# The last row's second layer in two groups of four K/V heads, each with its own softmax, under new instruction orders

## Chip, cores and metric

The kernel runs on one core of one Trainium2 chip. The metric is the device time of one execution in microseconds (us); lower is better. A time is given as the median of several executions, and one further execution was profiled.

## What is computed

Eight rows (one token each) go through four blocks: attention over a window of a K/V cache, a dense block, the same attention again with the same weights and caches, and the same dense block again. The window is the last 1024 of 4096 positions; there are 16 query heads and 8 K/V heads of 256 columns, so two query heads share a K/V head.

```python
def _A_ref(x, k_cache, v_cache, wq, wo):
    W = min(4096, max(256, Sk // 4))                     # 1024
    q = (x @ wq).reshape(B, Sq, Hq, Dh)...               # 8, 1, 16, 256
    k = jnp.repeat(k_cache[:, :, Sk - W:, :], rep, axis=1)
    v = jnp.repeat(v_cache[:, :, Sk - W:, :], rep, axis=1)
    p = _softmax(jnp.einsum("bhqd,bhkd->bhqk", q, k) * (Dh ** -0.5))
    return jnp.einsum("bhqk,bhkd->bhqd", p, v)... @ wo

x = x + _A_ref(_layernorm(x), A_k_cache, A_v_cache, A_wq, A_wo)
x = x + _B_ref(_layernorm(x), B_w1, B_w2)                # silu(x @ w1) @ w2
x = x + _A_ref(_layernorm(x), A_k_cache, A_v_cache, A_wq, A_wo)
x = x + _B_ref(_layernorm(x), B_w1, B_w2)
```

All data is bf16. K and V of the windows are 67 MB, the weights another 10.5 MB, and everything is read once.

## The kernel before, in words

**Stages of a row.** Each row b has two passes, called layer 1 and layer 2, that use the same K and V in SBUF. K/V pieces (512 KB each, 8 of K and 8 of V for a row) are loaded by SyncE into a ring of 30 slots (`load_kv`, L453; the order and the reuse of slots in `pump`, L1034). A slot is loaded again when the row's layer 2 has used it: K slots after the layer-2 scores, V slots after the layer-2 products with V. So TensorE's progress opens the gate for the loads of the next row but one.

- VectorE transposes K in place, two halves of each piece, 16 per row (`KT`, L630).
- Scores: TensorE multiplies the query blocks with K, in two halves of four K/V heads each (`S`, L645; 64 matmuls per layer and row, named S0 for layer 1 and S1 for layer 2, with .0 and .1 for the two halves). Both halves go into one PSUM bank, bank 0 for layer 1 and bank 1 for layer 2.
- Softmax (L654 to L676): VectorE takes the maximum and spreads it (max, mT, mg, mb: L658 to L662), ScalarE the exponential (`exp`, L664), TensorE a permutation (`perm`, L666), VectorE a transpose (`turn`, L668); TensorE sums the denominators (`l`, L671) and VectorE inverts them (`rl`, L676).
- Products with V (PV, L709 and L728), copies out of PSUM (`oev`, L698 and L703), a turn by matmuls with the identity (`oT`, L689), the division (`oTev`, L683), the product with wo (L781), a copy to a row (`rowb`, L1063), a fold of it into columns (`fold`, L499).
- Statistics of the row (`stat`, L814; `var`, L817; `pow`, L819), w1 (L516), a transpose (`yT`, L536), tanh (L826), `hT` (L827), w2 (L845), the same fold again, then the query product with wq (L872), its transpose (`qT`), `qm` (L881), `qd` (L885) and the query blocks for layer 2 (`qbd2`, L889).

Layer 1 of row b+1 needs only the input, so its scores, softmax and V products are woven between the stages of layer 2 of row b. For rows 0 to 6 the last output product and the second dense block are done together at the end (`final_rows`, L892), beside the last row's own chain; the last row is finished by `final_last` (L977). In the last row, layer 2's scores of all eight K/V heads go into bank 1, one softmax follows, then the V products of both halves, four copies of them on ScalarE (L698), the turns, and the product with wo (L781, `woL`).

**Zero products.** `busy` (L830) issues matmuls of 512 columns on a column of zeros: 8 in row 0, 5 in every other row, 5 more at the end. Their result is not used. They stand in TensorE's order at places where it would otherwise wait.

**Start.** Before the first use of wo and w2, sums of their rows are formed (`row_sums`, L426): three- and two-block reductions on VectorE (L435) and single ones on ScalarE (L443), with their writers L438 and L447. ScalarE loads its function table once at the start, and a second time by an explicit instruction (L328).

**Order.** Every engine runs its instructions in a fixed order. The steps are first listed in program order; the table `ORDER` (L16) then holds for each engine a string of digits, each of which says which of the steps that are left comes next. Waits on other engines are added by `emit` (L108). Nothing is chosen at run time: a step that waits holds up all that stands behind it on its engine.

Of the kernel before, what the change touches and what calls it, by code (L numbers as in the profile page):

```python
# [17 lines left out]
        "000000011111l111133312223022051002010033300710500300111117777000440033333210011004403330201101044000"  # L18
        "1770000300111117777000400444423010011155510022011101044000177005000011111777700040044442320001115514"
        "0022201101044000177710000011111777700040044442320001161514002201110004400017716111101111177770004004"  # L20
        "4442320001161510022201110105400017771000001111177770004004444232000116151002201111010033001777710100"
        "ccc0b1111060000444442200011817771002022220000033ccc43a02060500001140333333300110000022220b1200000000"
        "11000"),
    "dve": (
        "pSG0G0bGq0njnwvZtutFtUEg4CQz0g4yBydzjhvHwbvnFrEAAzkayz352iuj9k6q935nikb8g14f2a4439nj90888c8685c09664"
        "4551122baaa2a929216bd1aaa10077700555555000010098880870705ac09a90087700555550000100098880870705ac09aa"
        "0077700555550000100a08880878060aab09a0087700555550000100098880870705aa0aa90077700555550000100a088808"
        "78060aab0990087700555550000100098880778060acb0b99a900005555500000000099ag90ebb8ba8006004403020100001"
        "111100000000"),
    "act": (  # L30
        "13333442444455f5e56432322224222111111113312211111111111331211111111111133122111111111113312211111111"
        "11133122100000000000220111000000000302011000000004002200010010000000"),
    "pool": (
        "00010011022002200200020002000010001000"),
# [167 lines left out]
def bass_interleave_layers__sliding_block_cached__dense_activation_silu__decode_kernel(  # L202
# [429 lines left out]
    def scores(b, layer, k2):  # L632

        sc = bank[SC[layer]]
        q = qbd[layer][:]
        up_to = 8 if k2 else 16
        for cb in range(4):
            fns = []
            for par in range(2):
                for j in range(4):  # L640
                    a = 16 + 256 * k2 + (j * 8 + cb * 2 + par) * 8
                    w = q[:, a - up_to:a]
                    kv = slots[slot_of[b, "k", 4 * k2 + j]][:, :].rearrange(
                        "p (u cb jj par) -> p cb par u jj", u=8, cb=4, par=2)[:, cb, par, :, :]
                    fns.append(lambda e, w=w, j=j, kv=kv, cb=cb, par=par: e.matmul(  # L645
                        sc[32 * j:32 * j + up_to, 0:256], w, kv, start=(cb == 0 and par == 0),
                        stop=(cb == 3 and par == 1), tile_position=(0, 32 * j), skip_group_check=True))
            pe(fns, [k for j in range(4) for k in SL(slot_of[b, "k", 4 * k2 + j])] + [("pad", layer)] + QB(layer, k2),
               bk(SC[layer]), b, "S%d.%d" % (layer, k2))
# [4 lines left out]
    def softmax(b, L):  # L654
        m, tb = mm[L], LB[L]
        x = bank[SC[L]][:, 0:256]
        l_ps = bank[SC[L]][:, 256:256 + H]
        dve(lambda e: e.tensor_reduce(m[:, 0:1], x, AX.X, ALU.max, negate=True), bk(SC[L]), [("mm", L)], b, "max%d" % L)  # L658
        dve(lambda e: e.transpose(m[:], m[:]), [("mm", L)], [("mm", L)], b, "mT%d" % L)
        dve(lambda e: e.tensor_reduce(mg[L][:, 0:4], m[:, 0:16].rearrange("p (n q) -> p n q", q=4), AX.X,  # L660
                                      ALU.min), [("mm", L)], [("mg", L)], b, "mg%d" % L)
        dve(lambda e: e.transpose(m[:].rearrange("p (z n q) -> p z n q", z=2, q=4), view(mg[L][:], 0, [(0, 2), (1, 4), (0, 4)])),  # L662
            [("mg", L), ("mm", L)], [("mm", L)], b, "mb%d" % L)
        act(lambda e: e.activation(E_sb[L], x, ACTF.Exp, bias=m[:, 0:1], scale=1.0, accum_out=esum[:, L:L + 1]),  # L664
            bk(SC[L]) + [("mm", L)], QB(L, 1) + [("es", L)], b, "exp%d" % L)
        pe(lambda e: e.matmul(bank[tb][:, 0:256], perm[:], E_sb[L], start=True, stop=True),  # L666
           QB(L, 1) + PERM, bk(tb), b, "perm%d" % L)
        dve(lambda e: e.transpose(view(pT_sb[L], 0, [(64, 4), (1, 2), (2, 32)]),  # L668
                                  bank[tb][:, 0:256].bitcast(BF16)[:, 1:512:2].rearrange("p (u s n) -> p u s n", s=2, n=32)),
            bk(tb), QB(L, 0), b, "turn%d" % L)  # L670
        pe(lambda e: e.matmul(l_ps, esum[:, L:L + 1].broadcast_to([P, P]), selh[:], start=True, stop=True),  # L671
           [("es", L), "selh"], bk(SC[L]), b, "l%d" % L)
        if L == 1 and b < LAST:
            act(lambda e: e.activation(l2[b], l_ps, ACTF.Copy), bk(SC[L]), [("l2", b)], b, "lc1")
        else:
            dve(lambda e: e.reciprocal(rl[b], l_ps), bk(SC[L]), [("rl", b)], b, "rl%d" % L)  # L676

    def o_out(b, L, n, o_c, dst, h0, keys, name):
        if dst is None:
# [6 lines left out]
            bk(LB[L]) + [("rl", b)], keys, b, "oTev" + name)  # L686
# [6 lines left out]
    def o_turn(b, L, n, sel_o, o_c, dst, h0, keys, name, halves):  # L693

        ob = bank[OB[L]]
        if halves:
            for s in range(2):
                act(lambda e, s=s: e.activation(E_sb[L], ob[:, s * DH:(s + 1) * DH], ACTF.Copy), bk(OB[L]), QB(L, 1), b,  # L698
                    "oev%s.%d" % (name, s))
                o_sel(L, lambda s: E_sb[L], s, sel_o, o_c, n, QB(L, 1), b, "oT%s.%d" % (name, s))  # L700
# [4 lines left out]
        o_out(b, L, n, o_c, dst, h0, keys, name)  # L705

    def pv(b, L, j, kvh, u0, u1, c0, n, name, ob=None):

        return [lambda e, u=u: e.matmul(  # L709
            bank[OB[L] if ob is None else ob][32 * j:32 * j + 2 * n, :], pT_sb[L][:, pcol(u, c0):pcol(u, c0) + 2 * n],  # L710
# [39 lines left out]
    def pv_last2(b):  # L750
        for k2 in range(2):
            L = 1 - k2
            lists = [pv(b, 1, j, 4 * k2 + j, 0, 8, 2 + 8 * k2 + 2 * j, 2, "", OB[L]) for j in range(4)]
            for i in range(4):
                pe([l[i] for l in lists], [k for j in range(4) for k in SL(slot_of[b, "v", 4 * k2 + j])] + QB(1, 0),
                   bk(OB[L]), b, "PV1.%d" % k2)
            o_turn(b, L, 8, lambda s: view(ident[:], s, [(32, 4), (2, 2)]), C_O, oT2[b][:, :, 8 * k2:8 * k2 + 8], 8 * k2,
                   [("oT2", b, k2)], "L%d" % k2, True)
# [133 lines left out]
    def final_rows(s):  # L892
# [41 lines left out]
        for i0 in range(0, NCH, 8):  # L934
# [29 lines left out]
            bank[XB8][32 * (f % 4):32 * (f % 4) + n, 0:D], h8[:, f * n:(f + 1) * n],  # L964
            w2_sb[:, f // 2 * PW + R0 + f % 2 * D:f // 2 * PW + R0 + (f % 2 + 1) * D],
            start=(f < 4), stop=(f >= FC - 4), tile_position=(0, 32 * (f % 4)), skip_group_check=True)
            for f in range(FC)], ["h8"] + W2_R, bk(XB8), row, "w28")
# [3 lines left out]
        act(lambda e: e.activation(rb9, bank[XB8][:, 0:D], ACTF.Copy), bk(XB8) + KEY, ["rb8"], row, "rowb9")  # L971
# [158 lines left out]
```

## Time and profile before

| | us |
|---|---|
| median of 3 runs (235.59 to 236.86) | 236.27 |
| the profiled execution | 235.61 |
| its span in the profile | 233.7 |
| TensorE busy | 168.2 (72%) |
| VectorE busy | 155.3 (66%) |
| ScalarE busy | 68.5 (29%) |
| last K/V piece landed, about | 201 |

PE is TensorE, DVE VectorE, ACT ScalarE, POOL GpSimd, SP SyncE; SPq, PEq and so on are the engines' instruction queues. The chain of work that ended last is followed back from the last instruction: at each step to what released it, or to the instruction before it on its engine. In a timeline a row gives the start and the length in us, the engine, the line of the kernel, what is written and read, how many, and in brackets the idle time of the engine ahead of it with what ended that. The table of windows gives for each stretch its length, the busy time of each engine, TensorE's granted clock, the busy share of the DMA engines and the rate in GB/s. All times of a row count from the start of the span.

### The profile page before, as it was taken

Reading aid. Unit: us, or ns where it says so; the run is one execution under the profiler, and the core shown is the slowest. Engines: PE = TensorE matmul, PEld = TensorE weight load, DVE = VectorE, ACT = ScalarE, POOL = GpSimd, SP = SyncE. Lnnn points to the kernel's source line nnn. Section 1 sums busy time; section 2 is a strip of 40 time slices with the busy share of each in tenths; the row PEclk is TensorE's granted clock in tenths of the full one; section 3 lists DMA queues with packets and bytes.
Section 4 is the critical chain, followed back from the end, with each engine's and each line's share of the span. In section 5 each row is a group of like instructions: output and inputs, shape, how many; then the busy total and the mean of one; then the engine's idle time right before and its main releaser. Section 6 shows DMA issues by size and latency. Waiting matters only on the chain.

```text
span 233.7 us, 8070 instructions
## 1 busy us (share of the span) xinstructions
PE 168.2 (72%) x3569; PEld 93.4 (40%) x3569; DVE 155.3 (66%) x412; ACT 68.5 (29%) x205; POOL 22.8 (10%) x42
## 2 busy tenths in 40 slices
PE   0001505488788888989788898889788987999873
PEld 0001503123454455446344543644464454456441
DVE  3038999986963896488578649955974795365501
ACT  2000002896222321331332233225213322333330
POOL 1000022000300200200012001101010110012000
PEclk9999999999999999999999999999999999999999
DMA  6999999999999999999999999999999998300000
GB/s 163 413 403 407 379 381 399 407 407 412 405 403 392 414 404 356 365 414 409 400 406 406 400 400 409 409 326 407 410 406 382 411 409 329 127 3 3 3 1 4
DMA packets 23401, 78.20 MB, mean 335 GB/s; under 512 B 3127, under 2 KB 6086, under 8 KB 22982
## 3 DMA queue, kind: packets, MB, share of 16 engines
q1 hardware_dynamic: 22806, 77.30, 84.7%
q8 instruction: 28, 0.46, 0.8%
q10 hardware_dynamic: 560, 0.38, 0.8%
q14 instruction: 7, 0.06, 0.1%
HBM read 77.67 MB, written 0.01 MB: 332 GB/s over the span
## 4 chain that ended last, share of the span: by engine, by line
PE 47%; DVE 22%; DMA 13%; ACT 10%; issue 5%; SPq 2%; ACTq 0%; DVEq 0%
DMA slot<-in_A_k_cache_dram 13%; PE bank L645 11%; DVE slot L630 9%; PE bank L709 7%; PE bank L872 6%; PE bank L781 4%; DVE slot L435 3%; PE bank L845 2%; ACT qbd L664 2%; PE bank L728 2%; PE bank L516 2%; ACT slot L443 2%; PE bank L885 2%; ACT qbd L698 1%; PE bank L666 1%
## 5 line engine op out<-in xcount | busy, mean ns | idle before, releaser
L630 DVE STREAM_TRANSPOSE slot<-slot 128x512 uint32<-128x512 uint32 x128 | 81.9, 682 | 16.6 <-DMA slot<-in_A_k_cache_dram 16.3
L645 PE MATMUL bank<-slot,qbd 128*16 128x256 bf16 (+1 forms) x1024 | 40.4, 286 | 7.0 <-ACT qbd L889 3.2
L645 PEld LDWEIGHTS bank<-slot,qbd 128*16 128x16 bf16 (+1 forms) x1024 | 23.9, 88 | 17.8 <-ACT qbd L889 7.2
L709 PE MATMUL bank<-slot,qbd 128*4 128x512 bf16 (+1 forms) x384 | 27.9, 388 | 1.8 <-DVE xb L584 1.3
L819 POOL TENSOR_TENSOR fcols<-fcols 128x1 f32<-128x1 f32 x17 | 9.4, 553 | 109.6 <-ACT fcols L817 109.6
L781 PE MATMUL bank<-wo_sb,q1s 128*1 128x449 bf16 x284 | 17.0, 362 | 0.4 <-ACT wo_sb L447 0.4
L872 PE MATMUL bank<-wq_sb,xbz 128*2 128x256 bf16 x512 | 16.7, 275 | 0.1
L833 PE MATMUL bank<-ident,cols 128*128 128x512 bf16 x48 | 16.2, 391 | 0.0
L620 POOL TENSOR_TENSOR qbd<-q1s,fcols 128x256 bf16<-128x256 bf16 x16 | 9.6, 612 | 65.1 <-PE bank L689 59.1
L889 ACT ACTIVATE qbd<-bank 128x256 bf16<-128x256 f32 x16 | 6.1, 383 | 32.9 <-PE bank L885 32.9
L668 DVE STREAM_TRANSPOSE qbd<-bank 128x256 bf16<-128x256 bf16 x16 | 7.7, 478 | 12.1 <-PE bank L666 11.5
L683 DVE TENSOR_TENSOR q1s<-bank,q1s 128x16 bf16<-128x16 f32 (+1 forms) x18 | 2.9, 160 | 17.7 <-PE bank L689 17.5
L698 ACT ACTIVATE qbd<-bank 128x256 bf16<-128x256 f32 x22 | 8.3, 382 | 18.4 <-PE bank L709 16.8
L709 PEld LDWEIGHTS bank<-slot,qbd 128*4 128x4 bf16 (+1 forms) x384 | 8.1, 84 | 12.6 <-issue 2.1
L536 DVE STREAM_TRANSPOSE bank<-bank 128x256 f32<-128x256 f32 (+1 forms) x25 | 10.8, 433 | 3.6 <-PE bank L1004 1.2
L872 PEld LDWEIGHTS bank<-wq_sb,xbz 128*2 128x2 bf16 x512 | 11.4, 82 | 2.8 <-DVE xbz L807 0.4
L549 PE MATMUL bank<-xb,cols 128*128 128x8 bf16 x4 | 0.3, 173 | 16.6 <-DVE cols L331 16.6
L703 ACT ACTIVATE qbd<-bank 128x512 bf16<-128x512 f32 x14 | 8.3, 595 | 11.8 <-PE bank L728 10.9
L728 PE MATMUL bank<-slot,qbd 128*12 128x512 bf16 (+3 forms) x124 | 11.2, 408 | 0.0
L658 DVE TENSOR_REDUCE mm<-bank 128x1 f32<-128x256 f32 x16 | 6.8, 423 | 6.1 <-PE bank L645 5.4
L443 ACT ACTIVATE slot<-w_sb 128x448 bf16<-128x448 bf16 x6 | 3.5, 576 | 22.3 <-DMA w_sb<-in_B_w_dram 22.2
L845 PE MATMUL bank<-w_sb,q1s 128*1 128x449 bf16 x98 | 6.5, 353 | 4.8 <-DVE q1s L827 4.8
(158 smaller groups left out, 229.9 us busy)
## 6 DMA issues: line engine op xcount, KB each, us to landing
slot<-in_A_k_cache_dram SPq DMA_DIRECT2D x64, 512.0 KB, 8.5
slot<-in_A_v_cache_dram SPq DMA_DIRECT2D x64, 512.0 KB, 11.0
wo_sb<-in_A_wo_dram SPq DMA_DIRECT2D x1, 3584.0 KB, 25.5
wq_sb<-in_A_wq_dram SPq DMA_DIRECT2D x3, 1024.0 KB, 8.7
w_sb<-in_B_w_dram SPq DMA_DIRECT2D x1, 1568.0 KB, 27.8
w_sb<-in_B_w_dram SPq DMA_DIRECT2D x1, 1344.0 KB, 17.6
wq_sb<-in_A_wq_dram SPq DMA_DIRECT2D x1, 256.0 KB, 3.6
wq_sb<-in_A_wq_dram ACTq DMA_DIRECT2D x1, 256.0 KB, 4.0
```

What stands on the lines that cost most here:

```text
L536: dve(lambda e: e.transpose(view(bank[bi][:], n, [(2, n // 32), (n // 16, 16), (1, 2)]), bank[bi][:, 0:n].rearrange("p (g r s) -> p g r s" ...
L620: pool(lambda e, k2=k2: e.tensor_tensor(qdata(0, k2), q1s[:, b, 64 * k2:64 * k2 + 64].rearrange("p (n r) -> p n r", r=2).unsqueeze(3) .bro ...
L630: dve(lambda e, v=v: e.transpose(v, v), SL(s, h), SL(s, h), b, "KT%d" % k)
L645: fns.append(lambda e, w=w, j=j, kv=kv, cb=cb, par=par: e.matmul(sc[32 * j:32 * j + up_to, 0:256], w, kv, start=(cb == 0 and par == 0), st ...
L698: act(lambda e, s=s: e.activation(E_sb[L], ob[:, s * DH:(s + 1) * DH], ACTF.Copy), bk(OB[L]), QB(L, 1), b, "oev%s.%d" % (name, s))
L709: return [lambda e, u=u: e.matmul(bank[OB[L] if ob is None else ob][32 * j:32 * j + 2 * n, :], pT_sb[L][:, pcol(u, c0):pcol(u, c0) + 2 * n ...
L728: pe([lambda e, t=t, c0=c0, w=w, kvh=kvh: e.matmul(bank[OB[0]][32 * t:32 * t + 2 * w, :], pT_sb[0][:, pcol(2 * t, c0):pcol(2 * t, c0) + 2 ...
L781: fns.append(lambda e, i=i, w=w, c0=c0: e.matmul(bank[XB][32 * (i % 4):32 * (i % 4) + 1, c0:c0 + D + 1], oT(i), w, start=(i < 4), stop=(i ...
L819: pool(lambda e: e.tensor_tensor(rhalf, var4, nhalf, ALU.pow), ["var4", "nhalf"], ["rhalf"], b, "pow" + name)
L833: pe(lambda e: e.matmul(bank[SC[1]][:, :], cols[:, 3:4].broadcast_to([P, P]), view(ident[:], 0, [(0, 4), (1, P)]), start=True, stop=True), ...
L845: fns.append(lambda e, f=f, w=w, c0=c0: e.matmul(bank[XB][32 * (f % 4):32 * (f % 4) + 1, c0:c0 + D + 1], hTr[b][:, f:f + 1], w, start=(f < 4),
L872: pe([lambda e, j=j, c=c, s=s, wb=wb, k2=k2: e.matmul(bank[wb][32 * j:32 * j + 2, 0:256], pair(b, xcol(c, k2), s), view(wq_sb[:], c * HD + ...
```

## The change

In the last row, layer 2 is split at the half between K/V heads 3 and 4. The scores of the first half go into bank 1, those of the second into bank 0, and each half has a softmax of its own, with steps max, mT, mg, mb, exp, perm, turn, l and rl each; the denominators are kept apart. In the copies of the V products, each half's second copy moves from ScalarE to VectorE. Because bank 0 is now taken, w2 of the other seven rows (`w28`) uses bank 6. All zero products stay: 8, 5 and 5 as before. The strings of `ORDER` are new for all four engines; they move steps in every row, row 0 and the initial memsets included. Line numbers after L632 shift by 1 to 15.

```diff
-    def scores(b, layer, k2):
+    def scores(b, layer, k2, sb_i=None):
-        sc = bank[SC[layer]]
+        sb_i = SC[layer] if sb_i is None else sb_i
+        sc = bank[sb_i]
...
-    def softmax(b, L):
-        m, tb = mm[L], LB[L]
-        x = bank[SC[L]][:, 0:256]
-        l_ps = bank[SC[L]][:, 256:256 + H]
+    def softmax(b, L, g=None):
+        si, tb, qi = (SC[L], LB[L], L) if g is None else (SC[1 - g], LB[1 - g], g)
+        m, gm, E, pT = mm[si], mg[si], E_sb[qi], pT_sb[qi]
+        h0, nh = (0, H) if g is None else (8 * g, 8)
+        x = bank[si][:, 0:256]
+        l_ps = bank[si][:, 256 + h0:256 + h0 + nh]
...
     def o_turn(...)
             for s in range(2):
-                act(lambda e, s=s: e.activation(E_sb[L], ob[:, s * DH:(s + 1) * DH], ACTF.Copy), ...
+                if rk is None or s == 0:
+                    act(lambda e, s=s: e.activation(E_sb[qi], ob[:, s * DH:(s + 1) * DH], ACTF.Copy), ...
+                else:
+                    dve(lambda e, s=s: e.tensor_copy(pT_sb[qi], ob[:, s * DH:(s + 1) * DH]), ...
...
     def attend2(b):
         for k2 in range(2):
-            scores(b, 1, k2)
+            scores(b, 1, k2, SC[1 - k2] if b == LAST else None)
             freed.update((b, "k", 4 * k2 + j) for j in range(4))
             pump()
-        softmax(b, 1)
+            if b == LAST:
+                softmax(b, 1, k2)
+        if b < LAST:
+            softmax(b, 1)
```

Of `ORDER`, the first line of the string for VectorE, before and now:

```diff
-        "pSG0G0bGq0njnwvZtutFtUEg4CQz0g4yBydzjhvHwbvnFrEAAzkayz352iuj9k6q935nikb8g14f2a4439nj90888c8685c09664"
+        "nrAmnzFH.16jAv2HDvFjYuuhmCSCQsBfetOo2aIf91s944dCo26o1jdy9xk13igh59em0ak239g8g49d4838706k66696dd6ab11"
```

**VectorE, row 0.** What stands around row 0's first softmax before (L435 are the row sums of wo and w2, L658 to L662 are max to mb, L668 is turn):

```order
L435 TENSOR_REDUCE slot<-wo_sb 128x6 x2
L658 TENSOR_REDUCE mm<-bank 128x1
L331 MEMSET cols 1x1
L659 STREAM_TRANSPOSE mm<-mm 128x32
L660 TENSOR_REDUCE mg<-mm 128x4
L662 STREAM_TRANSPOSE mm<-mg 128x32
L435 TENSOR_REDUCE slot<-w_sb 128x4
L668 STREAM_TRANSPOSE qbd<-bank 128x4x2x32
```

The same place in the change (max to mb are now L663 to L667, turn is L673):

```order
L435 TENSOR_REDUCE slot<-wo_sb 128x6
L663 TENSOR_REDUCE mm<-bank 128x1
L664 STREAM_TRANSPOSE mm<-mm 128x32
L665 TENSOR_REDUCE mg<-mm 128x4
L435 TENSOR_REDUCE slot<-w_sb 128x4
L667 STREAM_TRANSPOSE mm<-mg 128x32
L435 TENSOR_REDUCE slot<-wo_sb 128x6
L438 TENSOR_SCALAR wo_sb<-slot 128x3x2
L673 STREAM_TRANSPOSE qbd<-bank 128x4x2x32
```

One of the two reductions ahead of max has moved behind mb, and the reduction of w2 from behind mb to ahead of it: between max and turn there are now two long reductions in place of one.

**TensorE, from row 6 to row 7.** Before, from the query product of row 6 (L872) to the first V products of row 7 (L709). L645 with 8x256 are here the second half of row 7's layer-1 scores, and with 16x256 and then 8x256 the two halves of row 6's layer-2 scores; L885 is qd, L666 perm of row 7's layer 1:

```order
L872 MATMUL bank<-wq_sb,xbz 2x256 x32
L645 MATMUL bank<-slot,qbd 8x256 x24
L885 MATMUL bank<-qm,spread 128x4x2x8 x4
L645 MATMUL bank<-slot,qbd 8x256 x8
L645 MATMUL bank<-slot,qbd 16x256 x32
L885 MATMUL bank<-qm,spread 128x4x2x8 x4
L666 MATMUL bank<-qbd,perm 128x256
L645 MATMUL bank<-slot,qbd 8x256 x32
L709 MATMUL bank<-slot,qbd 4x512 x16
```

In the change (L884 is the query product, L646 are the scores, L897 is qd, L671 perm, L721 the V products):

```order
L884 MATMUL bank<-wq_sb,xbz 2x256 x32
L646 MATMUL bank<-slot,qbd 8x256 x32
L897 MATMUL bank<-qm,spread 128x4x2x8 x8
L646 MATMUL bank<-slot,qbd 16x256 x32
L671 MATMUL bank<-qbd,perm 128x256
L646 MATMUL bank<-slot,qbd 8x256 x32
L721 MATMUL bank<-slot,qbd 4x512 x16
```

Both qd steps now stand together, ahead of all layer-2 scores, and nothing but perm stands between the halves of those.

**TensorE, the last row's layer 2.** Before, from the second half of the scores to the turns (L963 is w2 of the other seven rows, L968 and L972 belong to them too; L666 is perm, L671 l, L709 PV, L689 oT):

```order
L645 MATMUL bank<-slot,qbd 8x256 x32
L963 MATMUL bank<-w_sb,slot 7x448 x14
L968 MATMUL bank<-ident,slot 7x128 x3
L968 MATMUL bank<-ident,slot 7x64
L666 MATMUL bank<-qbd,perm 128x256
L671 MATMUL bank<-selh,fcols 128x16
L972 MATMUL bank<-slot 7x448
L709 MATMUL bank<-slot,qbd 4x512 x32
L689 MATMUL bank<-ident,qbd 128x8 x2
```

In the change (L671 is perm, L676 l, L721 PV, L695 oT):

```order
L646 MATMUL bank<-slot,qbd 8x256 x32
L975 MATMUL bank<-w_sb,slot 7x448 x14
L671 MATMUL bank<-qbd,perm 128x256
L980 MATMUL bank<-ident,slot 7x128 x3
L980 MATMUL bank<-ident,slot 7x64
L676 MATMUL bank<-selh,fcols 128x8
L984 MATMUL bank<-slot 7x448
L721 MATMUL bank<-slot,qbd 4x512 x4
L671 MATMUL bank<-qbd,perm 128x256
L721 MATMUL bank<-slot,qbd 4x512 x28
L676 MATMUL bank<-selh,fcols 128x8
L695 MATMUL bank<-ident,qbd 128x8 x4
```

There are two perm and two l; the second perm stands behind the first group of V products, and the turns of the first half follow together.

On ScalarE, the explicit table load (L328) moves from row 5, where it stood between the copy of the denominators (L674) and `rowb`, to row 7, between `var` (L829) and tanh (L838). In row 0, two of its reductions for w2 move from ahead of exp to behind it. On TensorE, in row 1 the turn of row 0's layer 2 (oT) stands ahead of the fold instead of behind it. In rows 2 and 3 (and, as before, row 6) the first half of the query product stands ahead of the layer-2 statistics step instead of behind it.

More of the change, by code (lines that the diff above doesn't have):

```diff
@@ L648, in scores @@
             pe(fns, [k for j in range(4) for k in SL(slot_of[b, "k", 4 * k2 + j])] + [("pad", layer)] + QB(layer, k2),
[L649 removed]
+               bk(sb_i), b, "S%d.%d" % (layer, k2))
     def pcol(u, c):
         return 64 * (u // 2) + 2 * c + u % 2
[L654 to L668 removed]
```

85 lines of the change are left out of this document (51 added, 34 removed).

## The prediction

> **What bounds the kernel now.** I read the page's shares of the chain of waits first.
>
> ```profile
> PE 47%; DVE 22%; DMA 13%; ACT 10%; issue 5%; SPq 2%; ACTq 0%; DVEq 0%
> ```
>
> Nearly half of the chain is TensorE and 13% are transfers. Two stretches of the table of windows (start:end, length, busy time of PE, PEld, DVE, ACT and POOL, granted clock, DMA share, GB/s) show what the middle rows are near to:
>
> ```profile
> 89.00:97.00 8.00, 6.64 (x125) 3.27 (x116) 3.39 (x12) 2.76 (x9) 0.00 (x0) 1.00 0.94 338
> 97.00:133.00 36.00, 31.15 (x688) 17.62 (x686) 28.17 (x66) 9.74 (x29) 4.59 (x8) 1.00 1.03 406
> ```
>
> TensorE is busy 31.15 of 36 us (87%) and the transfers run at 406 GB/s; only where slots come free late (89 to 97) do they drop to 338. A row has 16 pieces of 512 KB, 8.39 MB, which take 20.7 us at 406 GB/s. The rows follow each other at 21.2 us (the copy `rowb` of row 0 at 56.45 and that of row 5 at 162.34, both quoted below). So TensorE's order is the limit, with the transfers close behind: a shorter row cannot gain much before loading becomes the limit. SyncE's own waits say who holds the loads back (sum, number, longest):
>
> ```profile
> SPq L456 <- PE bank L645: 70.0, 12, 11.1
> ```
>
> They wait for scores, that is for TensorE to free K slots; a delay of TensorE in row 0 therefore delays loads too and is not made up by them. After about 201 us, when the last piece has landed, all is computation.
>
> **A, row 0: +1.6 (bounds +0.5 and +2.9).** The chain of waits through row 0's first softmax (start, length, engine, line):
>
> ```profile
> 36.96 5.72 DVE slot L435 x2
> 43.71 1.90 DVE slot L435
> 45.61 0.38 DVE qbd L668
> 46.04 1.45 PE bank L709 x12
> ```
>
> Before, max could start only when two reductions of wo had gone by, at 36.96 + 5.72 = 42.68, though the scores were done a little earlier. TensorE's timeline has the end of the scores, and further on row 0's two products with wo, which are needed below:
>
> ```profile
> 41.06 1.45 PE L645 MATMUL bank<-slot,qbd 128*8 128x256 bf16 x24
> ...
> 53.03 1.45 PE L781 MATMUL bank<-wo_sb,q1s 128*1 128x449 bf16 x16
> ...
> 55.46 0.93 PE L781 MATMUL bank<-wo_sb,q1s 128*1 128x449 bf16 x16 [0.41 <-ACT wo_sb L447]
> ```
>
> The scores ended at 42.51. I expect their end at about 41.1 now: the zero product of about 0.6 that stood between them is ahead of them, and VectorE hands over the query about 0.8 earlier (both estimates). From max to mb it was 42.68 to 43.71, 1.03, with 0.2 for mb: so max, mT and mg to 41.9, then the reduction of w2, 1.9, then mb, to 44.0 or 44.1. Behind mb now stands a reduction of wo, 5.72/2 = 2.9, where the shorter one of 1.9 stood: 47.0, a writer of about 0.2, and turn, 0.4, to 47.6. The V products start at 47.6 instead of 46.04: **+1.56**. ScalarE confirms it by another way:
>
> ```profile
> 42.61 0.58 ACT L443 ACTIVATE slot<-w_sb 128x448 bf16<-128x448 bf16 x1
> 43.09 0.19 ACT L443 ACTIVATION_READ_ACCUMULATOR slot<-w_sb 128x1 f32 x1
> 43.74 0.47 ACT L664 ACTIVATE qbd<-bank,mm 128x256 bf16<-128x256 f32 x1 [0.47 <-DVE mm L662]
> ...
> 56.45 0.55 ACT L1063 ACTIVATE rowb<-bank 128x450 bf16<-128x450 f32 x1 [1.13 <-PE bank L781]
> ```
>
> One of its reductions takes 0.67 with its read (42.61 to 43.28). Two of them move behind exp, 1.35 to 1.4, and exp starts at about 44.2 instead of 43.74, 0.46 later, so the last writer of wo's sums, for which the second product with wo waits (0.41 above), comes up to 1.9 later; some 0.3 of that goes into gaps between ScalarE's steps, which leaves 1.6. `rowb` would start at about 58.05, 1.6 later than before. The two ways agree, and nothing covers them: the rest of row 0 hangs on that `rowb`, and in TensorE's order row 1 begins only behind w2 of row 0. The low bound, +0.5, has only exp's own lateness (0.46) lost; the high one, +2.9, adds 1.3 for a slower TensorE. The rows for that are the zero products (line 833), by stretch:
>
> ```profile
> 50.00:54.00 4.00, 0.59 (x1) 0.10 (x1) 1.00 1.03 409
> 54.00:58.00 4.00, 1.14 (x3) 0.29 (x3) 1.00 1.03 410
> ```
>
> The same product took 0.59 in the first stretch and 1.14/3 = 0.38 in the second, at a granted clock (third number from the right) of 1.00 in both; the two products with wo above took 1.45 and 0.93 on the two sides of the change. If the lower rate of work lasted until row 0's first w1, the second product with wo would cost 0.5 more, and w1 with the zero products beside it, by the same ratio of 1.45/0.93, up to 0.8 more: together 1.3, an estimate. [...]
>
> **B, rows 1 to 5: −0.8 (0 and −1.5).** TensorE's waits at the statistics (sum, number, longest):
>
> ```profile
> PE bank L814 <- ACT q1s L867: 2.3, 5, 0.7
> ...
> PE bank L814 <- ACT q1s L680: 1.4, 5, 0.4
> ```
>
> The first row is for the layer-2 statistics, 2.3/5 = 0.46 each; the second the layer-1 statistics, 1.4/5 = 0.28 each, which wait for the copy (L680) of the turn of the row before, out of the same bank. Both together, 3.7, are the most that another order could hide. In row 1 that turn now stands ahead of the fold, so its copy is done when the statistics come: 0.3. In rows 2 and 3 half of the query product stands ahead of the layer-2 statistics and fills a wait of 0.46; `qm` needs the statistics' result, which comes later by this, so I take about half, 0.25 each. In rows 4 and 5 the same steps stand at nearly the same places. Sum −0.8. At worst it is nothing (what is put ahead delays the statistics' own chain by all that it fills); the upper end, −1.5, is 0.3 a row, since transfers of 20.7 us a row stand close behind.
>
> **C, row 6 to row 7: −0.4 (0 and −0.8).**
>
> ```profile
> 193.54 0.83 PE L645 MATMUL bank<-slot,qbd 128*8 128x256 bf16 x24 [0.70 <-DVE slot L630]
> ...
> 196.66 0.38 PE L885 MATMUL bank<-qm,spread 128*128 128x64 bf16 x4 [0.36 <-issue]
> ...
> 197.52 1.08 PE L645 MATMUL bank<-slot,qbd 128*8 128x256 bf16 x32 [0.32 <-ACT qbd L889]
> ```
>
> With both qd steps together, ScalarE's copies of the query blocks run beside the first half of the scores: the wait of 0.32 ahead of the second half and some of the 0.36 ahead of the second qd go. I take −0.4 of the 0.68; the upper end, −0.8, adds a little of the 0.70 ahead of 193.54. At the least it is nothing: both qd must now be done before any layer-2 score. VectorE puts the first transposes of row 7's K ahead of a division of row 6, which can cost 0.7 if that K lands late; the same 0.70 of idle time at 193.54 would cover it.
>
> **D, the last row's tail: −0.7 (+0.3 and −1.1).** The end of the chain:
>
> ```profile
> 216.19 1.72 PE bank L645 x52
> 217.93 0.43 DVE mm L658
> ...
> 220.61 1.93 PE bank L709 x32
> 222.56 0.39 ACT qbd L698
> 223.25 0.39 ACT qbd L698
> 223.89 1.66 PE bank L781 x24
> ```
>
> One softmax lay wholly between the scores and the V products: 217.91 to 220.61, 2.7 us. Now max of the first half starts when its 32 matmuls are through. Half of the scores is some 1.0 us (the row at 197.52), so max at about 216.95, and the same 2.7 us, with w2 of the other rows beside it, give 219.7; with 0.15 for the smaller engine order I take 219.85 for the first V products (before 220.61). Half of them last 0.97, to 220.8. The second max cannot start before the scores' end and its turn stands behind one more VectorE step:
>
> ```profile
> 220.59 0.61 DVE L974 CAST slot<-bank 7x448 bf16<-7x448 f32 x1
> ```
>
> That puts the second half's V products at 220.9, their end at 221.9 instead of 222.54, so −0.6. Of the four copies (223.25 is the last of them), half go to VectorE, beside ScalarE: the last copy ends 0.1 sooner after the products than its 1.1 us before, and the product with wo starts at about 223.1 to 223.2 instead of 223.89. **−0.7.** Added are one max, mT, mg, mb, exp, perm, turn, l and rl: some 2 us of VectorE and ScalarE, in stretches where these wait for scores anyway. Without that cover the second chain starts when the first is through with VectorE and the V products of the second half are 1 us later than taken: +0.3. The other end is −1.1, the 0.97 of one half fully hidden and 0.1 from the copies.
>
> **E, ScalarE's table load: 0 (0 and +0.43).**
>
> ```profile
> 160.56 1.28 ACT L328 ACT_TABLE_LOAD   x1
> 162.34 0.55 ACT L1063 ACTIVATE rowb<-bank 128x450 bf16<-128x450 f32 x1 [0.50 <-PE bank L781]
> ...
> 208.86 0.27 ACT L826 ACTIVATE th<-bank,fcols 128x14 f32<-128x14 f32 x1 [1.35 <-DVE bank L536]
> ```
>
> It moves to just ahead of tanh of row 7, where ScalarE waits 1.35 for w1's transpose. 1.28 fits. If what stands around it costs as much as the 0.50 left after it in row 5, 1.28 + 0.50 − 1.35 = 0.43 is late, on the path. [...]
>
> **Sum.** +1.6 − 0.8 − 0.4 − 0.7 + 0 = **−0.3** on the profiled execution's 235.61: 235.3. The median of the runs is 0.66 above that execution, so on its scale the prediction is **236.0**, by −0.3 from 236.27.
>
> **Rivals.** *R1, the delay of row 0 does not reach the end: 234.4.* Row 0's excess would be taken up if rows 1 and 2 are held by their K and V rather than by TensorE: 236.27 − 0.8 − 0.4 − 0.7 = 234.4. For it speaks the 338 GB/s at 89 to 97, a place where loads are late; against it that SyncE waits for TensorE (70.0 us over 12). *R2, slower: row 0's delay comes with longer products on TensorE and the middle rows gain nothing: 238.1.* [...] Price: 1.6 + 1.3 − 0.4 − 0.7 = +1.8, 238.1. It decides for slower as soon as these longer products cost over 0.7, with nothing from the middle rows. [...] *R3, the table load is not hidden: 237.3.* If it starts only when tanh could have started, all of its 1.28 is late: 236.0 + 1.3. Against it: in row 5 it started as soon as ScalarE was free, and 0.50 is all that is seen behind it. [...] *R4, the second softmax doesn't shorten the tail: 236.7.* This is the change not doing what it says: the second max, exp and turn are served behind the first half's on VectorE and ScalarE, so the second V products start where the only ones did, and D is 0. Against it speaks that VectorE has little else there.
>
> **How the numbers follow.** The forecast, within some 0.7 of 236.0, has 0.42; R1 0.26; R2 0.20; R4 0.07; R3 0.05. A measurement of this kernel can tell about 0.5%, 1.2 us: faster is below 235.1, slower above 237.4. R1 is faster, and 0.04 of the forecast's case: 0.30. R2 is slower (0.20), with it half of R3, which lies at the bound (0.03), and 0.04 of the forecast's case: 0.27. What is left is 0.43. The range goes from 234.0 (R1 with 0.4 more from the middle rows) to 238.2 (R2). Outside lie A at its high bound with C or D at their low ones too, and a saving in row 0 with all gains at their upper ends.
>
> **What would show it.** A: the V products of row 0 start at about 47.6 and not near 46.0, and `rowb` near 58.0; B: the sum of TensorE's waits at the statistics falls from 3.7 by about 0.8, and the second half of row 7's layer-1 scores starts at about 194.3 (193.54 + 1.6 − 0.8); C: the wait of 0.32 ahead of the second half of the scores is gone; D: from the last scores' end to the product with wo less than 5.4 us instead of 223.89 − 217.91 = 6.0; E: tanh of row 7 starts within 0.4 us of its operand. The prediction is wrong if row 0's V products start at 46 or earlier, if the zero products in row 0 take 0.59 up to the first w1, or if the second turn of the last row waits long behind VectorE's other steps.

## The result and the profile after

The change is a little faster: 234.56 us median of 6 runs (233.92 to 234.72), against 236.40 for the kernel before (235.59 to 237.00), ratio 0.9914 with a 95% interval of 0.9889 to 0.9938. A second comparison gave 0.9948 (0.9917 to 0.9980). The profiled execution took 234.59, with a span of 232.80, against 235.61 and 233.72 before: 1.02 less of its own time, 0.92 less in the span.

The chain of waits of the changed kernel, in shares by engine:

```profile
PE 57%; DVE 19%; ACT 9%; issue 6%; DMA 5%; SPq 1%; POOL 1%; DVEq 0%; ACTq 0%
```

TensorE has more of it than before (57% for 47%) and transfers less (5% for 13%); that alone says nothing about time. The stages do. The first transpose of K, which starts when the first K piece has landed, in VectorE's timeline of before and of after:

```profile
15.49 0.71 DVE L630 STREAM_TRANSPOSE slot<-slot 128x512 uint32<-128x512 uint32 x1 [12.21 <-DMA slot<-in_A_k_cache_dram]
```

```profile
15.96 0.71 DVE L630 STREAM_TRANSPOSE slot<-slot 128x512 uint32<-128x512 uint32 x1 [12.89 <-DMA slot<-in_A_k_cache_dram]
```

The profiled execution of after thus started 0.47 later. The kernel before, profiled once more below, started at 16.07, so this much differs without a change. Over all fourteen profiles of this document the starts are 15.49 to 16.33 where the first rows are ordered as before and 15.96 to 16.86 where they are ordered as in the change; a small part of the change in it is neither shown nor excluded. The copy `rowb` of rows 0 and 5 (L1075 now) in ScalarE's timeline of after, then the last row's layer-2 scores and the product with wo in TensorE's timeline of before and of after:

```profile
57.12 0.55 ACT L1075 ACTIVATE rowb<-bank 128x450 bf16<-128x450 f32 x1 [1.13 <-PE bank L793]
...
163.30 0.55 ACT L1075 ACTIVATE rowb<-bank 128x450 bf16<-128x450 f32 x1 [1.66 <-PE bank L793]
```

```profile
216.12 1.76 PE L645 MATMUL bank<-slot,qbd 128*16 128x256 bf16 x56
...
223.82 1.69 PE L781 MATMUL bank<-wo_sb,q1s 128*1 128x449 bf16 x32
```

```profile
216.69 1.60 PE L646 MATMUL bank<-slot,qbd 128*16 128x256 bf16 x48
...
224.03 1.69 PE L793 MATMUL bank<-wo_sb,q1s 128*1 128x449 bf16 x32
```

And the end of the program, SyncE's timeline and its wait for the output, before and then after:

```profile
230.36 0.62 SPq L1021 DMA_DIRECT2D out_dram<-slot  x1
```

```profile
SPq L191 <- DMA out_dram<-slot: 2.2, 1, 2.2
```

```profile
230.61 0.62 SPq L1033 DMA_DIRECT2D out_dram<-slot  x1
```

```profile
SPq L191 <- DMA out_dram<-slot: 1.0, 1, 1.0
```

Read together, stage by stage (start to start in us; the scores' end is the end of the last score matmul, 217.88 and 218.28 in the trace):

| stage | before | after | difference |
|---|---|---|---|
| start to first K | 15.49 | 15.96 | +0.47 |
| to `rowb` of row 0 | 40.96 | 41.16 | +0.20 |
| to `rowb` of row 5 | 105.89 | 106.18 | +0.29 |
| to the last scores' end | 55.54 | 54.98 | −0.56 |
| to the product with wo | 5.94 | 5.75 | −0.19 |
| to the issue of the output | 6.54 | 6.58 | +0.04 |
| from there to the end | 3.36 | 2.19 | −1.17 |

When the output is issued the changed kernel is still 0.25 **behind**. All of its gain, 1.17, lies in the last 3 us, where nothing that the output needs is computed any more: the same transfer of the same row of output is waited for 2.2 us before and 1.0 us after. No term of the prediction speaks of it. What moved on the DMA queues in the stretch from 229 to the end, before and after:

```profile
q8 instruction: 1, 0.02, 0.5%
q14 instruction: 1, 0.01, 0.2%
```

```profile
q8 instruction: 1, 0.02, 0.8%
```

Before, one more load of instructions (8 KB, queue 14) stands there. Its packet starts at 231.83 and takes 0.31; three of the four output packets of 224 bytes start at 231.62 to 231.65, the fourth at 232.14, just as that load is through, and SyncE goes on at 233.20. After, the last load on queue 14 is at 224.10, the four packets start within 0.06, and SyncE goes on 1.67 after the issue, as the times of the single packets and instructions in the two traces say.

### The profile page after: what moved, and what is told of

The parts are those of the page before. It is cut to its first block, busy times and chain, and to the rows that moved or that the text cites. A ratio compares the mean times of both kernels' runs of the same rounds, so it can differ in the third digit from the quotient of the medians.

```text
span 232.8 us, 8081 instructions
## 1 busy us (share of the span) xinstructions
PE 168.5 (72%) x3572; PEld 93.2 (40%) x3572; DVE 157.3 (68%) x420; ACT 68.2 (29%) x205; POOL 22.8 (10%) x42
## 4 chain that ended last, share of the span: by engine, by line
PE 57%; DVE 19%; ACT 9%; issue 6%; DMA 5%; SPq 1%; POOL 1%; DVEq 0%; ACTq 0%
PE bank L646 12%; PE bank L721 10%; DVE slot L630 7%; PE bank L793 6%; DMA slot<-in_A_k_cache_dram 5%; PE bank L884 5%; PE bank L740 4%; PE bank L516 3%; PE bank L857 3%; PE bank L695 2%; DVE slot L435 2%; PE bank L671 2%; PE bank L897 2%; PE bank L845 2%; PE bank L826 2%
## 5 line engine op out<-in xcount | busy, mean ns | idle before, releaser
L646 PE MATMUL bank<-slot,qbd 128*16 128x256 bf16 (+1 forms) x1024 | 39.6, 286 | 5.6 <-ACT qbd L901 2.8
L721 PE MATMUL bank<-slot,qbd 128*4 128x512 bf16 (+1 forms) x384 | 28.3, 389 | 3.4 <-DVE qbd L673 3.2
L646 PEld LDWEIGHTS bank<-slot,qbd 128*16 128x16 bf16 (+1 forms) x1024 | 22.9, 88 | 16.4 <-ACT qbd L901 6.4
L884 PE MATMUL bank<-wq_sb,xbz 128*2 128x256 bf16 x512 | 17.0, 275 | 0.7 <-DVE xbz L819 0.7
L901 ACT ACTIVATE qbd<-bank 128x256 bf16<-128x256 f32 x16 | 6.1, 382 | 32.3 <-PE bank L897 29.9
L845 PE MATMUL bank<-ident,cols 128*128 128x512 bf16 x48 | 15.1, 386 | 0.0
L706 ACT ACTIVATE qbd<-bank 128x256 bf16<-128x256 f32 x20 | 7.6, 382 | 19.9 <-PE bank L721 17.4
L673 DVE STREAM_TRANSPOSE qbd<-bank 128x256 bf16<-128x256 bf16 x17 | 8.1, 475 | 7.9 <-PE bank L671 7.7
L721 PEld LDWEIGHTS bank<-slot,qbd 128*4 128x4 bf16 (+1 forms) x384 | 7.8, 84 | 13.5 <-DVE qbd L673 3.4
L884 PEld LDWEIGHTS bank<-wq_sb,xbz 128*2 128x2 bf16 x512 | 11.3, 82 | 3.1 <-DVE xbz L819 0.8
L689 DVE TENSOR_TENSOR q1s<-bank,q1s 128x16 bf16<-128x16 f32 (+1 forms) x18 | 2.8, 157 | 13.4 <-PE bank L695 13.4
L663 DVE TENSOR_REDUCE mm<-bank 128x1 f32<-128x256 f32 x17 | 7.1, 417 | 6.1 <-PE bank L646 5.8
L793 PEld LDWEIGHTS bank<-wo_sb,q1s 128*1 128x1 bf16 x284 | 6.6, 85 | 8.4 <-DVE q1s L689 2.2
L669 ACT ACTIVATE qbd<-bank,mm 128x256 bf16<-128x256 f32 x17 | 8.0, 471 | 4.8 <-DVE mm L667 4.8
```

Source lines behind the costliest of these rows:

```text
L673: dve(lambda e: e.transpose(view(pT, 0, [(64, 4), (1, 2), (2, 32)]), bank[tb][:, 0:256].bitcast(BF16)[:, 1:512:2].rearrange("p (u s n) -> ...
L721: return [lambda e, u=u: e.matmul(bank[OB[L] if ob is None else ob][32 * j:32 * j + 2 * n, :], pT_sb[L if qi is None else qi][:, pcol(u, c ...
L793: fns.append(lambda e, i=i, w=w, c0=c0: e.matmul(bank[XB][32 * (i % 4):32 * (i % 4) + 1, c0:c0 + D + 1], oT(i), w, start=(i < 4), stop=(i ...
L845: pe(lambda e: e.matmul(bank[SC[1]][:, :], cols[:, 3:4].broadcast_to([P, P]), view(ident[:], 0, [(0, 4), (1, P)]), start=True, stop=True), ...
L884: pe([lambda e, j=j, c=c, s=s, wb=wb, k2=k2: e.matmul(bank[wb][32 * j:32 * j + 2, 0:256], pair(b, xcol(c, k2), s), view(wq_sb[:], c * HD + ...
```

## The experiments

**Theory (store):** the gain is that load. VectorE's instructions come in loads of 8 KB (seven single ones on queue 14 during the run); in the kernel before, one of them falls on the end of its program, at 231.83, and delays the output. The change has ten more records on VectorE, that is instructions in its trace (458 for 448: the second softmax, two copies and two that only wait or signal), which moves the load away. **Rival (orders):** the gain is in the stages, and the profiled executions happen to differ at the end. All ratios are to the kernel before.

**b_again**, the kernel before without a change.

> The kernel before, once more, against itself: a second profile of it, and what the comparison gives for no change. In the first profile the output transfer was issued at 230.36 and SyncE went on at 233.20, 2.84 us later; in the changed kernel these were 230.61 and 232.29, 1.68 us. Theory (store): a load of VectorE's code falls on the end of the program and one of the four output packets stands behind it; then the 2.8 us come again. Rival (chance): the store's time varies from execution to execution; then about 1.7 us are as likely. The time stays within 0.3% either way.

Ratio 1.0003 (0.9978 to 1.0028). The store theory's case came: the load on queue 14 at 231.86, and the wait again twice that of after:

```profile
SPq L191 <- DMA out_dram<-slot: 2.0, 1, 2.0
```

From the issue to SyncE's going on it was 2.61 us, and again the fourth packet started when the load ended (232.36, and 231.86 + 0.51). The stages up to the issue also show what one kernel varies by: first K at 16.07 instead of 15.49, and 55.34 instead of 55.54 from `rowb` of row 5 to the scores' end.

**b_pad10**, the kernel before with ten idle-time memsets; nothing else differs.

```diff
+    for _ in range(10):
+        const(eps4, 4.0 * EPS, ["eps4"], name="dummy")
     const(eps4, 4.0 * EPS, ["eps4"])
```

> The kernel before with ten more one-element-wide memsets on VectorE, written twice over with the same value, in its idle time before the first K piece. They move the place of VectorE's code loads by ten instructions, as the change does (458 records of VectorE for 448), and nothing else. Theory (store): the last load of VectorE's code comes near 224 us instead of 231.8, the output transfer takes 1.7 instead of 2.8 us, and the time falls by about 1.1 us, 0.5%. Rival (orders): the gain of the change is in the stages; then the time stays as before within 0.2%.

Ratio **0.9931** (0.9906 to 0.9955), 234.54 us median: about the whole gain of the change, from ten instructions that compute nothing. The load moved to 218.73, the output took 1.67 us, and the wait is that of after:

```profile
SPq L191 <- DMA out_dram<-slot: 1.0, 1, 1.0
```

Since only VectorE's program grew, it is VectorE's load. The rival falls as the main cause. Counted in the traces, a load starts behind the 442nd to 451st record of VectorE in all fourteen profiles; in before, with 448 records, that is the end, and in b_pad10 it is behind the 443rd of 458.

**a_pad54, a_end and a_end2** try the opposite, to bring the load back to the end of the changed kernel, with 54, 118 and 119 memsets (in the diff of b_pad10 with 54, or with 94 and the rest, 24 or 25, in idle time of row 7 and the end; here a_end2):

```diff
     def attend2(b):
+        for _ in range(25 if b == LAST else 0):
+            dve(lambda e: e.memset(rl[b][:, 0:1], 0.0), [], [("rl", b)], b, "late")
         for k2 in range(2):
```

> The changed kernel with 54 such memsets in VectorE's idle time before the first K piece, so that the records of VectorE are 512, again a multiple of 64 as the 448 of before, and the load falls on the end again. Theory (store): 2.8 us for the output transfer and 1.1 us more than the changed kernel, so about 235.7 and a gain on before of only 0.3%. Rival (orders): the same 234.6 as the changed kernel.

> The changed kernel with 118 tiny memsets more on VectorE, 94 in its idle time before the first K piece and 24 in its idle time of row 7 and the end, so that its records are 576 = 448 + 128 and the load of VectorE's code that stands near 224 us comes at the very end, as in the kernel before. The 94 end at about 15 us, the first transpose is at 16. Theory (store): the output transfer takes 2.6 to 2.8 us instead of 1.68, and the time is about 235.7, 1.1 us above the changed kernel and within 0.4% of before. Rival (orders): the changed kernel's time, 234.6, with at most 0.2 for the memsets.

> As a_end with one tiny memset more (119). In a_end the code load came at 235.18, 1.1 us after VectorE's very last instruction, too late to meet the output. One instruction earlier it comes about 1.3 us after VectorE's last work, as in the kernel before. Theory (store): the output transfer takes 2.6 to 2.8 us instead of 1.67. Rival: 1.67 again.

The first two missed their aim. The guess of a load at every 64 records (seven in 448 before) was wrong: in a_pad54 the last load came behind the 447th of 512 records, at 203.39, far from the end. In a_end the last came behind all 575 records, at 235.18, after the end. Both outputs took 1.67 us, so their ratios (0.9954, 0.9925 to 0.9984, and 0.9956, 0.9925 to 0.9987) say nothing on the store. In a_end2, one memset more, the load came behind the 575th of 576 records, at 232.42 for 0.31; one of the four packets again started only when it had ended (232.73, 0.26 behind the third), and the output took 2.59 us. This is one execution, of 236.18 us, without a ratio of its own:

```profile
SPq L192 <- DMA out_dram<-slot: 2.0, 1, 2.0
```

So the delay of 0.9 to 1.2 us follows the load's place in both kernels: with the load at the output 2.83, 2.61 and 2.59 us from issue to going on, without it 1.67 or 1.68 in all eleven other profiles. By the ratios b_pad10 gains 1.6 us (1.1 to 2.2), the change 2.0 (1.5 to 2.6) in the first comparison and 1.2 (0.5 to 2.0) in the second. Only the first comparison of the change lies above the 1.2 of the load, and what it has beyond that is not explained.

**ab_early**, the code of before in the changed orders of rows 0 to 7 up to the last layer-2 scores, with ten memsets. Of its order on TensorE, against that of before and with the line numbers of before, at row 0's scores:

```diff
 L600 MATMUL bank<-slot 128x16x2 x16
+L833 MATMUL bank<-ident,cols 128x512
 L645 MATMUL bank<-slot,qbd 16x256 x32
-L645 MATMUL bank<-slot,qbd 8x256 x8
-L833 MATMUL bank<-ident,cols 128x512
-L645 MATMUL bank<-slot,qbd 8x256 x24
+L645 MATMUL bank<-slot,qbd 8x256 x32
```

> The code of before with one softmax in the last row's layer 2, in the changed orders up to the last row's layer-2 scores and in those of before behind them, and ten tiny memsets more on VectorE so that the code load is away from the end as in b_pad10 (ratio 0.9931). It shows the new orders of rows 0 to 7 alone. Theory (orders cost): the traces have the changed kernel 0.2 to 0.5 us later than before at the last row's layer-2 scores for the same arrival of the first K piece; then the ratio is 0.994 to 0.995. Rival (the forecast's A + B + C = +0.4 is outweighed, orders gain 0.4): ratio 0.9915.

Ratio 0.9952 (0.9928 to 0.9976), on the side of "orders cost", 0.2% above b_pad10, though the intervals overlap. The rival, that the orders gain 0.4 us, is excluded by the interval only just; no stage shows a gain: 41.16 to `rowb` of row 0 (40.95 to 40.96 in three profiles of before), 106.21 to that of row 5 (105.79 to 106.13).

**bt_tail, best1, best2 and a_act** take the tail apart. bt_tail has the orders of before up to the last layer-2 scores and the changed ones behind; best1 moves exp, perm, turn and the other rows' sum besides; best2 keeps the changed order there. In a_act (the changed kernel), best1 and best2 the second half's second copy is on ScalarE:

```diff
-                    dve(lambda e, s=s: e.tensor_copy(pT_sb[qi], ob[:, s * DH:(s + 1) * DH]), ...
+                    if name == "L1":
+                        act(lambda e, s=s: e.activation(pT_sb[qi], ob[:, s * DH:(s + 1) * DH], ACTF.Copy), ...
+                    else:
+                        dve(lambda e, s=s: e.tensor_copy(pT_sb[qi], ob[:, s * DH:(s + 1) * DH]), ...
```

> The changed kernel with the second copy of the second half of the last row on ScalarE, behind the first, instead of on VectorE. In the changed kernel this copy starts at 223.41, after two reciprocals and a division, and the last turn waits 0.63 us for it. Theory (copy): on ScalarE it starts at about 223.0, the product with wo starts at 223.6 instead of 224.03, and the time falls by 0.4 us, to about 234.2. Rival (the chain is held elsewhere): no change, 234.5 to 234.6.

> The code of the changed kernel, with the orders of before up to the last row's layer-2 scores (VectorE up to its max, ScalarE up to its exp) and all of GpSimd's, and the changed orders behind them: the second softmax and the copies alone. Theory (store): the code load is away from the end, 1.1 us; the tail itself gains 0.2 us from the scores' end to the product with wo (5.94 before, 5.74 in the changed kernel); in all about 1.3 us, ratio 0.9945 to before. Rival (the forecast's D): 0.7 us from the tail besides, 1.8 us, ratio 0.992.

> As bt_tail, and with the second copy of the second half on ScalarE, the second exp right behind the first, the second perm ahead of all V products, the second turn right behind the first, and the sum of the other rows' output (L984) behind the first group of V products. Theory (D was held by these places): from the scores' end to the product with wo 5.1 us or less instead of 5.74, so 0.8 us from the tail and 1.1 from the store: ratio 0.992 to before, the best of all. Rival (the tail is held by the 64 matmuls and the first softmax alone): no more than bt_tail.

> The orders of before up to the last row's layer-2 scores on every engine, VectorE's up to the step ahead of max; behind them the changed orders, with the second copy of the second half on ScalarE as in a_act. In best1 and bt_tail max had stood behind a step of the other rows (0.4 us late), and in best1 the sum of the other rows held the second V products for 0.70. Theory (the tail can give what was forecast): max 0.9 us before the scores' end, 5.1 to 5.2 us from the scores' end to the product with wo (5.94 before), output transfer 1.67, the scores' end as in before; ratio to before 0.990 to 0.992. Rival (the tail gives nothing once the code load is away): b_pad10's ratio, 0.993.

The stage from the scores' end to the product with wo:

| kernel | stage | ratio to before |
|---|---|---|
| before | 5.94 | |
| changed | 5.75 | 0.9914 (0.9889 to 0.9938), 0.9948 (0.9917 to 0.9980) |
| a_act | 5.11 | 0.9930 (0.9905 to 0.9955) |
| bt_tail | 6.13 | 0.9969 (0.9946 to 0.9992) |
| best1 | 6.44 | 0.9983 (0.9956 to 1.0011) |
| best2 | 5.12 | 0.9934 (0.9901 to 0.9967) |

The stage of a_act is as its theory had it, 0.64 shorter than in the changed kernel. In the changed kernel VectorE's second copy stands behind two reciprocals and a division, and TensorE's last turn waits for it, as these rows of VectorE's and TensorE's timelines of after show:

```profile
223.41 0.42 DVE L710 CAST qbd<-bank 128x256 bf16<-128x256 f32 x1 [0.21 <-issue]
```

```profile
223.89 0.21 PE L695 MATMUL bank<-ident,qbd 128*128 128x8 bf16 x2 [0.63 <-DVE qbd L710]
```

In a_act ScalarE does the copy right behind the first, at 223.25 with scores that ended 0.43 later, and the turns need no wait:

```profile
222.97 0.38 ACT L706 ACTIVATE qbd<-bank 128x256 bf16<-128x256 f32 x1 [0.56 <-PE bank L725]
223.25 0.38 ACT L711 ACTIVATE qbd<-bank 128x256 bf16<-128x256 f32 x1
```

The theory of best1 fell by my own order. The second group of V products writes the bank of the other rows' sum (L988) and waited for the copy of that sum (L990):

```profile
222.86 1.03 PE L725 MATMUL bank<-slot,qbd 128*4 128x512 bf16 x16 [0.70 <-DVE slot L990]
```

and, as in bt_tail, the orders of before had put a step of the other rows ahead of the first max, which then started at 217.90 instead of the 217.39 of the changed kernel. best2 mends both and reaches 5.12. But its ratio and a_act's are not below those of b_pad10 (0.9931) and of the change: **0.6 to 0.8 us are won in the stage and do not show beyond the intervals**, each about ±0.3%. The profile of best2 can't say where they go: its execution, of 236.85, is the longest of twelve with a median of 234.32, and its rows alone took 108.21 from `rowb` of row 0 to that of row 5.

bt_tail and best1 missed their theories. Both outputs took 1.67 us, and still their ratios lie above the 0.9945 and 0.992 that were expected, and above b_pad10's by 0.9 and 1.2 us. Their stages explain 0.2 and 0.5 of that (6.13 and 6.44 for 5.94); the intervals leave room for the rest, which is open.

No version beat the changed kernel beyond the intervals.

**a_row3**, the changed kernel with the statistics of rows 2 and 3 where they stood before; its order on TensorE against that of the change, in row 3:

```diff
-L516 MATMUL bank<-w_sb,xbz 2x224 x32
-L826 MATMUL bank<-xbz 128x1 x4
+L826 MATMUL bank<-xbz 128x1 x4
+L516 MATMUL bank<-w_sb,xbz 2x224 x32
...
-L884 MATMUL bank<-wq_sb,xbz 2x256 x32
-L826 MATMUL bank<-xbz 128x1 x4
-L884 MATMUL bank<-wq_sb,xbz 2x256 x32
+L826 MATMUL bank<-xbz 128x1 x4
+L884 MATMUL bank<-wq_sb,xbz 2x256 x64
```

> The changed kernel with TensorE's layer-1 statistics of row 3 ahead of w1 again, and the layer-2 statistics of rows 2 and 3 ahead of the query product again, as before. From row 3 to row 4 the changed orders take 21.70 us (S0.1 to S0.1) where before takes 21.29. Theory (B turned round): those statistics stand too late, 0.4 us come back at row 4 and the last row's scores end 0.2 to 0.4 us earlier; ratio to before about 0.2% below the changed kernel's. Rival (transfers): row 3 waits for K and V, and nothing is gained.

Ratio 0.9976 (0.9952 to 1.0000), not below the change. From row 3's second scores to row 4's it took 21.59 instead of 21.70, and the row ahead 21.62 instead of 21.28: nothing came back, and the theory that these statistics cost the rows 0.4 falls. That transfers hold row 3 is not shown either; in this profile TensorE waits for no K or V directly.

**a_again**, the changed kernel once more.

> The changed kernel once more, in five rounds against before. The kernel before with its code load moved (b_pad10) came to a ratio of 0.993, the first comparison of the change to 0.991. Theory (store alone): rows and tail of the change give and take alike, so its ratio is that of b_pad10, 0.993, and its output transfer takes 1.67 us again. Rival (the orders and the second softmax give something besides): 0.991 or less again.

0.9948 (0.9917 to 0.9980), output 1.67 us, and all stages within 0.25 us of the first profile of the change (41.27, 105.94, 55.03, 5.73). The store theory's 0.993 lies in both intervals of the change, the rival's 0.991 in the first alone; that the change gives more than b_pad10 is not shown.

## Why the prediction was right and where it was wrong

The time lay in the range (234.0 to 238.2) and on the forecast's side, but not by the sum: −1.8 on the medians where −0.3 was forecast, and the largest part of it from a place the sum did not have. That the range held it is luck: its low end was set by R1, which is not what happened.

- **What was left out, −1.2.** The sum was set "on the profiled execution's 235.61", so what follows the last instruction was carried over as a constant, without a word. The profile of before had the row that could have raised the question, 2.2 us of waiting for an output of 0.9 KB, and queue 14 in its last 4 us. b_pad10, b_again and a_end2 show that the load of VectorE's code makes 0.9 to 1.2 us.
- **A, +1.6 forecast, +0.2 measured.** The mechanism was right: two reductions between max and turn. These pieces of the chain of after show them (start, length, engine, line):

```profile
36.68 3.62 PE bank L646 x33
...
41.20 1.93 DVE slot L435
43.13 0.12 DVE mm L667
43.25 2.84 DVE slot L435
...
46.70 1.90 PE bank L721 x13
```

  1.93 and 2.84 against my 1.9 and 2.9. What failed is "their end at about 41.1", that of the scores: they began at 36.68, 1.6 before those of before and not 0.8, and ended at 40.27, so the V products came at 46.70 instead of 47.6. Counted from the first K piece that is 30.74 against 30.55, the 0.2 that `rowb` shows too. The second way, by ScalarE's reductions, agreed with the first only because it took its exp time from it (44.2; it was 43.28, and the first `rowb` 57.12 instead of 58.05).
- **B, −0.8 forecast, no gain measured.** The waits at the statistics did shrink, from 2.3 + 1.4 and 0.3 behind a third step to 2.7 in all (L826 here), and others took their place. TensorE's waits at the first turn before, then its waits after:

```profile
PE bank L689 <- ACT qbd L698: 3.1, 10, 0.6
```

```profile
PE bank L695 <- ACT qbd L706: 3.3, 7, 0.5
...
PE bank L826 <- DVE xbz L819: 1.2, 3, 0.6
PE bank L826 <- ACT q1s L879: 1.0, 2, 0.7
...
PE bank L884 <- DVE xbz L819: 0.7, 2, 0.3
...
PE bank L826 <- ACT q1s L686: 0.5, 2, 0.4
```

  Half of the query product ahead of the statistics now waits for the same columns itself (0.7, L884), and in rows 1 to 6 the first turn behind the V products waits 0.49 (most of the 3.3), where before it was 0.17 in rows 2 to 6 (the 3.1 of before lies mostly in rows 0, 1 and 7): the sum of the denominators (`l`, L671 before) had stood between the V products and that turn, and now stands behind it. From `rowb` of row 0 to that of row 5 it took 105.89, 105.79 and 106.13 in three profiles of before, and 106.18, 105.94 and 106.19 in those of the change, a_again and a_act. The step "I take about half" counted what filled the named waits and not what had filled the waits from which it was taken.
- **C, −0.4 forecast, −0.56 in the profiles, with E in it.** One profile of before with the memsets has 55.01 in this stage without any of C, so it is not more than the scatter. In the trace the parts are as told: the 0.32 ahead of the second half of row 6's scores is gone, but the second qd waits 0.56 (0.36 before):

```profile
196.14 0.38 PE L897 MATMUL bank<-qm,spread 128*128 128x64 bf16 x4 [0.56 <-ACT qbd L901]
```

- **D, −0.7 forecast, −0.2 measured.** The first half was as forecast: max 0.9 before the scores' end. The size failed at "half go to VectorE, beside ScalarE": the second copy there was worth +0.6, which a_act gives back (5.11). One of the signs that the prediction had named for being wrong did come: the last row's turn waits 0.63 for a copy that stands behind VectorE's other steps.
- **E, 0 forecast, +0.2 measured.** Tanh started right behind the load, at 209.23:

```profile
207.93 1.28 ACT L328 ACT_TABLE_LOAD   x1
209.23 0.27 ACT L838 ACTIVATE th<-bank,fcols 128x14 f32<-128x14 f32 x1
```

  Its operand was there at about 209.0, so it cost 0.2. Between the load's end and tanh lie 0.02 us.
- **The rivals.** R1's 234.4 was met, for another reason than R1's. R2's longer products did not come in the profile of the change: the second product with wo took 0.93 there (at 56.13), as before. What does come in five of the fourteen profiles (b_again, bt_tail, best2, a_row3, a_again) is a granted clock below 0.7 in a stretch of row 0 (0.50 to 0.66 from 44, in best2 from 46, to 52); there `rowb` of row 0 came 0.0 to 0.5 us later from the first K piece than in the others of the same order, not the 1.3 of R2's sum, which no run shows.

## What to carry to other kernels

Here a gain under 1% came from where a load of instructions falls (ratio 0.9931 in b_pad10, with ten memsets as the only change): before a small change is credited to its idea, pad the engine whose program it lengthened by as many empty instructions, and look at the wait for the last output. Carry the time behind the last instruction as a term of its own. And a step put into a wait has left a gap where it stood: count both.

## What the runs showed of the hardware

- A load of VectorE's code of 8 KB in the last 2 us lengthened the output's 1.67 us to between 2.59 and 2.83, by 0.9 to 1.2 us (before, b_again, a_end2). In all three cases one of the four output packets started just when the load ended. Less than half of the delay is the packet that starts late (0.26 to 0.5); what the rest is stays open.
- The medians of before and after differ by 1.8 us in the first comparison and by 0.8 in the second, the profiled executions by 1.0; both profiles of before lie 0.5 to 0.8 below their medians. What lengthens the other executions of before is open.
- The granted clock fell in some executions of the same kernel in row 0 and not in others: from 44 to 52 it was 1.00 in the profile of before and 0.59 in b_again, the same kernel (the column behind the busy times):

```profile
44.00:52.00 8.00, 4.55 (x47) 1.90 (x51) 7.81 (x11) 7.58 (x28) 0.00 (x0) 0.59 1.02 406
```

- The first K piece was there between 15.49 and 16.86 us in fourteen profiles, and such a difference need not last: b_again was 0.58 behind before at the first K and 0.29 at the issue of the output.
